# Another order of the same units in a fused attention and gated-MLP kernel

## The chip, the cores and the metric

The kernel runs on one core of a Trainium2 chip. The metric is the device time of one execution in microseconds, as the median of three executions: 165.45 us before the change (165.12 to 165.77). A profile of one execution is read beside it; its span is 164.6 us.

Five engines of the core run side by side, each with its own list of instructions that it takes in order: TensorE (PE in the profile, with its weight loads as PEld), VectorE (DVE), ScalarE (ACT), GpSimd (POOL) and SyncE (SP). GpSimd and SyncE also issue the DMA transfers.

## The reference, cut to what matters

Four batches, eight heads, a sequence of 768 and a head dimension of 64. Keys and values are mixed between eight blocks of 96 rows by a small matrix P that five rounds of normalization make nearly doubly stochastic; then comes attention inside each block, and then a gated MLP whose gate mixes the whole sequence.

```python
P = sort_net                                   # (4, 8, 8, 8)
for _ in range(5):
    P = np.exp(P - P.max(-1, keepdims=True))
    P = P / (P.sum(-1, keepdims=True) + 1e-9)
    P = P / (P.sum(-2, keepdims=True) + 1e-9)
k_sb = einsum("bhij,bhjcd->bhicd", P, k_b)     # blocks of k and of v, mixed
v_sb = einsum("bhij,bhjcd->bhicd", P, v_b)
attn = softmax(q_b @ k_sb.T / 8)               # inside each block of 96
x = attn @ v_sb                                # heads side by side: (4, 768, 512)
h = relu(x @ w_in)                             # w_in: 512 x 1024
u, v = h[..., :512], h[..., 512:]
v_n = (v - mean(v)) / sqrt(var(v) + 1e-6)
v_s = einsum("ts,bsd->btd", w_spatial, v_n) + b_spatial[None, :, None]
out = (u * v_s) @ w_out
```

## The kernel before

The kernel is a list of units, the string ORDER. Each unit is a small function that emits the instructions of one piece of work on the engines concerned, and the string is walked from left to right. So the order in the string is the order of the instructions on each engine; between engines only data and buffers tie them together. The arguments after a unit's name are mostly the PSUM bank, the engine that copies the result (A ScalarE, D VectorE, P GpSimd), the batch and the piece.

The units, in the words that this document uses:

- `L`, `LH`: a load of q, k or v of a batch (`LH` of half the heads), or of a weight (`wv` and `wu` the two halves of w_in, `ws` w_spatial, `wo` w_out). GpSimd issues all of them. q, k and v have two buffers each, so batch 2 reuses the buffers of batch 0.
- `SK`: a round of the normalization of P (exponential on ScalarE, the rest on VectorE); the last one also gives its transpose p_t. `PR`: the products that spread P over the partitions. `P0`: the masked mixing weights of batch 0, on VectorE. `PD`: those of the other batches, on GpSimd.
- `DM`: dummy matmuls on a tile of zeros whose result nobody reads.
- `QT`: transposes of q. `KT`, `VT`: mixing and transposing k, and v of batch 0. `VX`, `VM`, `VC`: the way of v into the layout that attention wants, `VC` being copies from SBUF to SBUF that SyncE issues. `QX`: transposing q of batches 2 and 3 by DMA.
- `SC`: scores and their exponential. `AT`: attention times v and its division (with P, ScalarE copies first and GpSimd multiplies). `XT`, `XX`: transposing x on TensorE, or by DMA.
- `VP`, `LN`, `LA`: the v half of h and its normalization. `UP`: the u half. `WS`: transposes of w_spatial. `SP`, `SH`: the product with w_spatial, the bias and the gate. `OP`, `OH`: the product with w_out, and the store.
- `WT`: a copy of one element on GpSimd, which makes GpSimd wait for a transposed tensor before it issues what stands behind.

The parts that the change and the prediction touch, with the order's first lines (cuts are marked):

```python
ORDER = """
IN LH:q:0:0:4 L:k:0:0:128 ID SK:0 MK SK:0 SK:0 QT:0:D:0:0:2 IV:1 QT:2:A:0:1:2 SK:0 DM:2:12:192
DM:0:12:192 SK:1 DM:2:12:192 SX DM:0:12:192 IV:0 PR:2 P0:1:0:4 L:v:0:0:128 P0:0:0:4 P0:1:4:8 P0:0:4:8
PC:A DM:7:5:384 KT:0:A:0:1:2 KT:3:D:0:0:2 ...
"""                                            # cut: 29 more lines

def load(x, b, lo, hi):
    src = {"q": q, "k": k, "v": v}[x]
    if (x, b) not in st:
        alloc(b, x)
    nc.gpsimd.dma_start(
        out=st[x, b][lo:hi],
        in_=_raw_ap(src, b * H * S * D + lo * G * D, [[G * D, hi - lo], [S * D, H], [1, G * D]]),
    )

def u_DM(ps, n, w):
    t = ps_tile(ps)
    for _ in range(int(n)):
        nc.tensor.matmul(t[:, 0, 0:int(w)], lhsT=warm[:, 0:128], rhs=warm[:, 0:int(w)], start=True, stop=True)

def u_PR(ps):
    st["pr"] = ps_tile(ps)[:, 0, 0:NB * BH].rearrange("p (x i y) -> p x i y", x=2, i=NI)
    for ih in range(2):
        for ii in range(NI):
            nc.tensor.matmul(
                st["pr"][:, ih, ii, :], lhsT=sel[:, ii, :], rhs=p_t[:, ih, :], start=True, stop=True)

def u_P0(ih, lo, hi):
    ih, lo, hi = int(ih), int(lo), int(hi)
    n = hi - lo
    pr = st["pr"][:, ih]
    nc.vector.tensor_mul(
        out=pd[0][:, lo:hi, ih * 64:ih * 64 + 64].rearrange("p h (i t) -> p h i t", t=TB),
        in0=_raw_ap(mask16, 0, [mask16.ap[0], [0, n], [0, NI], [1, TB]]),
        in1=_raw_ap(pr, lo, [pr.ap[0], [1, n], [BH, NI], [0, TB]]),
    )

def u_PD(b, lo, hi):
    b, lo, hi = int(b), int(lo), int(hi)
    n = hi - lo
    nc.gpsimd.tensor_mul(
        out=pd[b][:, lo:hi].rearrange("p h (i t) -> p h i t", t=TB),
        in0=_raw_ap(mask16, 0, [mask16.ap[0], [0, n], [0, NB], [1, TB]]),
        in1=_raw_ap(prep_sb, b * H + lo, [prep_sb.ap[0], [1, n], [BH, NB], [0, TB]]),
    )

def u_QT(ps, eng, b, hp, ih):
    b, hp, ih = int(b), int(hp), int(ih)
    lo, n = (0, 128) if ih == 2 else (ih * 64, 64)
    t = ps_tile(ps).rearrange("p x c -> p (x c)")
    for g in range(G):
        for hh in range(2):
            nc.tensor.matmul(
                t[hh * 64:hh * 64 + 64, g * n:(g + 1) * n],
                lhsT=st["q", b][lo:lo + n, 2 * hp + hh, g * D:(g + 1) * D],
                rhs=ident[lo:lo + n, lo:lo + n],
                start=True, stop=True,
            )
    copy(
        eng,
        q_tile(b, hp)[:, lo * G:(lo + n) * G].rearrange("p (x g) -> p x g", g=G),
        t[:, 0:n * G].rearrange("p (g x) -> p x g", g=G),
    )

# ... cut: KT, VT, VX

def u_VM(ps, eng, b, hp):
    b, hp = int(b), int(hp)
    t = ps_tile(ps)
    for hh in range(2):
        nc.tensor.matmul(
            t[:, hh, 0:G * D], lhsT=pd[b][:, 2 * hp + hh, :], rhs=st["v", b][:, 2 * hp + hh, :],
            start=True, stop=True,
        )
    copy(
        eng,
        vm[b % 2][:, :, 2 * hp:2 * hp + 2, 0:D].rearrange("p g h d -> p h g d"),
        t[:, :, 0:G * D].rearrange("p h (g d) -> p h g d", g=G),
    )

def u_VC(b, ih):
    b, ih = int(b), int(ih)
    for i in range(ih * NI, ih * NI + NI):
        src = vm[b % 2][i * TB:(i + 1) * TB]
        dst = vb[b % 2][:, i]
        nc.sync.dma_start(
            out=dst.rearrange("c h d -> c (h d)"),
            in_=src.rearrange("t g h d -> t g (h d)"),
        )

def u_WT(x, b, ih):
    b, ih = int(b), int(ih)
    src = st["qX", b][0:1, 0, 0:1] if x == "q" else x_tile(b, ih)[0:1, 0, 0:1]
    nc.gpsimd.tensor_copy(out=gate[0:1, 0:1], in_=src)

def u_OH(ps, eng, b, c):
    b, c = int(b), int(c)
    t = ps_tile(ps)
    for mc in range(FC):
        nc.tensor.matmul(
            t[:, 0, :], lhsT=st["gt", b, mc][:, c * 128:(c + 1) * 128], rhs=w_out_sb[:, mc, :],
            start=(mc == 0), stop=(mc == FC - 1),
        )
    o_sb = moe.tile([128, DM], FP32, name="oh_sb", tag="oh", bufs=3)
    copy(eng, o_sb, t[:, 0, :])
    nc.sync.dma_start(out=out[b, c * 128:(c + 1) * 128, :], in_=o_sb)
```

Of the kernel before, what the change touches and what calls it, by code (L numbers as in the profile page):

```python
# [13 lines left out]


ORDER = """
IN LH:q:0:0:4 L:k:0:0:128 ID SK:0 MK SK:0 SK:0 QT:0:D:0:0:2 IV:1 QT:2:A:0:1:2 SK:0 DM:2:12:192
DM:0:12:192 SK:1 DM:2:12:192 SX DM:0:12:192 IV:0 PR:2 P0:1:0:4 L:v:0:0:128 P0:0:0:4 P0:1:4:8 P0:0:4:8
PC:A DM:7:5:384 KT:0:A:0:1:2 KT:3:D:0:0:2 KT:5:A:0:3:2 VT:2:A:0:1 LH:q:0:4:8 VT:7:D:1:1 L:wv
VT:0:D:2:1 SC:3:0:1:1 KT:5:D:0:2:2 VX:7:A:0:1 VX:0:D:1:1 SC:1:0:0:1 QT:3:A:0:2:2 VT:7:D:2:0 PD:3:0:4  # L20
AT:5:D:0:1:1 VT:0:A:3:1 QT:1:A:0:3:2 PD:1:4:8 L:wu VX:7:D:2:1 AT:3:D:0:0:1 L:ws PD:3:4:8 SC:5:0:2:1
VX:0:A:3:1 VX:7:D:2:0 VT:1:D:0:0 SC:3:0:3:1 AT:5:D:0:2:1 VT:7:D:1:0 L:v:1:0:128 VT:0:A:3:0 SC:1:0:1:0
AT:3:D:0:3:1 XT:5:D:0:1:0 PD:2:0:4 SC:6:0:0:0 VX:0:A:0:0 L:k:1:0:128 VX:1:D:3:0 PD:1:0:4 PD:2:4:8
VX:2:A:1:0 XT:3:D:0:1:1 SC:6:0:2:0 AT:4:D:0:0:0 SC:0:0:3:0 L:q:1:0:128 VP:3:A:0:5 AT:6:P:0:2:0
VP:4:D:0:3:4 L:wo AT:6:P:0:3:0 WS:0:A:2 UP:2:A:0:1:1 AT:4:D:0:1:0 WS:0:A:1 UP:6:A:0:0:1 L:v:2:0:128
VM:2:D:1:0 VM:0:A:1:3 XT:4:D:0:0:0 WS:5:A:5 L:k:2:0:128 XT:7:D:0:0:1 VM:2:A:1:1 LN:0:3:6 VM:0:D:1:2
L:q:2:0:128 WS:4:D:3 L:v:3:0:128 VP:7:A:0:2 KT:0:A:1:0:2 KT:2:A:1:2:2 KT:4:A:1:3:2 LA:P:0:5
VP:6:A:0:0:1 WS:0:A:0 UP:4:A:0:1:0 QT:6:D:1:3:2 LN:0:0:3 QT:2:A:1:1:2 LA:P:0:4 VC:1:1 QT:0:D:1:2:2
UP:4:A:0:0:0 KT:6:D:1:1:2 SC:2:1:3:1 QT:0:D:1:0:2 LA:P:0:3 SC:4:1:2:1 LA:P:0:0 SC:6:1:1:1 WS:2:D:4
VC:1:0 AT:0:D:1:3:1 LA:P:0:1 SC:4:1:0:1 AT:2:D:1:2:1 BB SC:6:1:1:0 VM:0:A:2:0 AT:4:D:1:1:1 SC:6:1:0:0  # L30
AT:2:D:1:0:1 LA:P:0:2 AT:0:P:1:1:0 SC:4:1:3:0 AT:6:D:1:0:0 SP:2:D:0:1 SC:6:1:2:0 XX:1:1 AT:4:P:1:3:0
SP:0:P:0:0 AT:4:P:1:2:0 VM:6:A:2:2 QX:D:2 SP:2:D:0:3 VM:4:A:2:1 XX:1:0 VM:6:A:2:3 VC:2:1 VC:2:0
SP:0:D:0:2 WT:x:1:0 L:k:3:0:128 VM:6:A:3:0 VM:2:A:3:1 VM:4:D:3:2 UP:0:A:1:0:1 UP:2:A:1:1:1
KT:0:D:2:2:2 KT:4:A:2:3:2 KT:6:A:2:1:2 KT:2:D:2:0:2 VM:0:A:3:3 OP:4:D:0:2 SC:0:2:0:1 SC:2:2:3:1
VP:6:A:1:4:5 AT:2:P:2:3:1 AT:0:P:2:0:1 L:q:3:0:128 VP:4:D:1:0:1 SC:2:2:3:0 SC:6:2:2:0 LN:1:4:6
VP:0:A:1:2:3 SC:6:2:1:1 SC:4:2:1:0 LA:P:1:5 OP:2:A:0:1 LA:P:1:4 AT:6:D:2:3:0 OP:0:A:0:0 AT:2:D:2:2:0
AT:4:P:2:1:0 UP:6:D:1:0:0 LN:1:0:4 VC:3:0 SC:2:2:0:0 SC:4:2:2:1 UP:0:A:1:1:0 LA:D:1:1 LA:D:1:2
AT:2:D:2:0:0 KT:6:A:3:3:2 LA:D:1:0 LA:P:1:3 KT:4:A:3:2:2 XX:2:0 KT:0:D:3:1:2 KT:2:A:3:0:2 QX:D:3
SP:6:D:1:2 AT:2:P:2:1:1 AT:0:D:2:2:1 SP:4:D:1:0 SP:6:P:1:1 VP:0:D:2:0:1 UP:4:A:2:1:0 SP:6:D:1:3
SC:4:3:0:0 SC:0:3:2:0 XX:2:1 VP:2:D:2:2:3 SC:0:3:1:0 SC:4:3:2:1 UP:6:A:2:0:0 AT:0:D:3:0:0 LN:2:0:4  # L40
VP:2:A:2:4:5 UP:6:A:2:1:1 LA:P:2:2 AT:0:P:3:2:0 AT:2:P:3:1:0 LA:D:2:1 LA:D:2:3 UP:4:A:2:0:1 LN:2:4:6
LA:D:2:0 SC:0:3:3:0 LA:D:2:5 VC:3:1 SC:6:3:0:1 LA:P:2:4 OP:2:D:1:2 OP:4:A:1:1 AT:2:D:3:3:0 XX:3:0
AT:6:D:3:2:1 SP:0:P:2:1 SC:6:3:1:1 SC:2:3:3:1 OP:4:A:1:0 AT:2:D:3:1:1 AT:6:D:3:0:1 SP:0:P:2:3
AT:2:D:3:3:1 XX:3:1 UP:6:D:3:0:0 SP:0:D:2:2 UP:6:A:3:1:0 SP:0:D:2:0 VP:6:A:3:0:1 VP:0:A:3:2:3
OP:6:A:2:1 LN:3:0:4 LA:D:3:1 VP:0:A:3:4:5 LA:D:3:2 UP:6:A:3:1:1 LN:3:4:6 LA:P:3:5 UP:2:A:3:0:1
LA:P:3:3 LA:D:3:4 LA:D:3:0 OP:6:A:2:2 OP:0:D:2:0 SP:6:D:3:1 SP:0:D:3:2 SP:6:P:3:0 SH:0:D:3:3:0
SH:1:D:3:3:1 OH:0:A:3:0 OH:7:A:3:2 OH:1:A:3:1 OH:0:A:3:3 OH:7:A:3:4 OH:1:A:3:5
"""


# [593 lines left out]
```

## Time and profile before

| what | value |
|---|---|
| time, median of 3 | 165.45 us |
| span of the profiled execution | 164.6 us |
| TensorE busy | 145.4 us (88%), 1593 matmuls |
| VectorE busy | 112.4 us (68%) |
| ScalarE busy | 87.3 us (53%) |
| GpSimd busy | 56.0 us (34%) |
| DMA packets | 36690, 25.50 MB |

How to read it: [...] The chain of waits is followed back from the last instruction, at each step to what released it. A line such as L289 is a line of the kernel: L261 `PR`, L268 `P0`, L280 `PD`, L289 `DM`, L296 `WS`, L323 `QT`, L338 `KT` and `VT`, L389 `VM`, L422 `SC`, L447 `AT`, L535 `UP`, L547 `SP`, L582 `OH`; L107 and L109 are the helper that copies on ScalarE and on VectorE, and L155 the helper of the loads.

### The profile page before, as it was taken

What the parts mean: (1) busy time and instruction counts of PE and PEld (TensorE: products, weight loads), DVE (VectorE), ACT (ScalarE), POOL (GpSimd) and SP (SyncE); (2) the same over time, 40 slices, a digit from 0 to 9 for tenths busy, and PEclk for the clock granted to TensorE, in tenths of its full rate; (3) what the DMA queues carried; (4) which work ended last, traced back from release to release, by engine and by line L of the source; (5) the groups of instructions that cost most, each with busy time, mean ns of one, the idle gap of its engine ahead of it and who ended that gap; (6) DMA issues with size and microseconds to landing.
All of it is one profiled execution on the core that took longest, in us unless ns stands there. A gap on an engine that the chain in (4) does not pass through costs nothing.

```text
span 164.6 us, 3884 instructions
## 1 busy us (share of the span) xinstructions
PE 145.4 (88%) x1593; PEld 91.5 (56%) x1593; DVE 112.4 (68%) x225; ACT 87.3 (53%) x135; POOL 56.0 (34%) x77
## 2 busy tenths in 40 slices
...
GB/s 16 202 203 204 81 137 208 205 203 205 209 250 255 203 201 191 130 192 95 203 239 204 312 189 199 105 4 0 0 295 187 96 0 0 131 127 127 0 208 178
DMA packets 36690, 25.50 MB, mean 155 GB/s; under 512 B 16576, under 2 KB 33472, under 8 KB 36672
## 3 DMA queue, kind: packets, MB, share of 16 engines
...
q8 instruction: 12, 0.20, 0.5%
q14 instruction: 6, 0.05, 0.1%
...
## 4 chain that ended last, share of the span: by engine, by line
PE 62%; DMA 21%; DVE 7%; ACT 3%; issue 2%; SPq 1%; POOLq 1%; POOL 1%; ACTq 0%; DVEq 0%
PE ps L547 14%; DMA v_in<-in_v_dram 10%; PE ps L490 10%; PE ps L535 10%; PE ps L596 7%; PE ps L289 4%; PE ps L447 4%; PE ps L422 4%; DMA xT<-x_sb 4%; DMA q_in<-in_q_dram 3%; DMA vb<-vm 3%; DVE z L553 2%; PE ps L338 2%; PE ps L582 2%; PE ps L389 2%
## 5 line engine op out<-in xcount | busy, mean ns | idle before, releaser
L547 PE MATMUL ps<-wspT,v_sb 128*128 128x384 bf16 x180 | 32.0, 332 | 0.0
L435 ACT ACTIVATE ex<-ps 96x768 bf16<-96x768 f32 x32 | 24.6, 806 | 10.7 <-PE ps L422 10.6
L535 PE MATMUL ps<-xT,w_in_sb 128*128 128x384 bf16 x128 | 23.1, 326 | 1.2 <-DVE z L553 1.1
L547 PEld LDWEIGHTS <-v_sb 128*128 128x128 bf16 x180 | 17.5, 100 | 11.6 <-issue 0.8
L459 POOL TENSOR_TENSOR x_sb<-xr,rec 96x512 bf16<-96x512 f32 x11 | 11.7, 1069 | 34.6 <-DVE rec L458 30.6
L490 PE MATMUL ps<-w_in_sb,xT 128*128 128x512 bf16 x96 | 22.7, 380 | 0.0
L504 DVE BATCH_NORM_STATS2 stats<-v_sb 128x6 f32<-128x512 bf16 x24 | 16.3, 679 | 9.1 <-ACT v_sb L113 8.9
L113 ACT ACTIVATE u_sb<-ps 128x768 bf16<-128x768 f32 x14 | 11.3, 809 | 17.8 <-PE ps L535 10.2
L553 DVE TENSOR_TENSOR z<-ps,b_bc 128x768 f32<-128x768 f32 x15 | 14.3, 955 | 7.3 <-PE ps L547 7.3
L535 PEld LDWEIGHTS <-w_in_sb 128*128 128x128 bf16 x128 | 11.9, 98 | 9.2 <-issue 1.3
L596 PE MATMUL ps<-w_out_sb,gt 128*128 128x512 bf16 x72 | 16.7, 379 | 0.0
L459 DVE TENSOR_TENSOR x_sb<-ps,rec 96x512 bf16<-96x512 f32 x21 | 14.4, 687 | 0.7
L559 POOL TENSOR_TENSOR gt<-z,u_sb 128x768 bf16<-128x768 f32 x5 | 8.2, 1643 | 17.9 <-DVE z L553 17.9
L490 PEld LDWEIGHTS <-xT 128*128 128x128 bf16 x96 | 8.7, 98 | 9.3
L447 PE MATMUL ps<-vb,ex 96*128 96x65 bf16 x256 | 12.6, 197 | 1.2 <-DMA vb<-vm 1.2
L447 PEld LDWEIGHTS <-ex 96*128 96x128 bf16 x256 | 11.0, 100 | 4.6 <-issue 1.6
L521 POOL TENSOR_SCALAR v_sb<-v_sb,nm,rstd 128x512 bf16<-128x512 bf16 x13 | 10.5, 811 | 3.9 <-ACT rstd L512 2.5
L596 PEld LDWEIGHTS <-gt 128*128 128x128 bf16 x72 | 6.7, 98 | 7.5
L113 ACT ACTIVATE v_sb<-ps 128x1024 bf16<-128x1024 f32 (+1 forms) x9 | 8.4, 931 | 4.2 <-PE ps L490 4.0
L520 POOL TENSOR_SCALAR nm<-mv 128x1 f32<-128x1 f32 x13 | 2.7, 207 | 22.2 <-DVE mv L505 22.2
L422 PEld LDWEIGHTS <-kT 64*96 64x96 bf16 x256 | 7.8, 122 | 4.3 <-issue 3.3
L280 POOL TENSOR_TENSOR pd<-mask,prep_sb 128x512 bf16<-128x512 bf16 x6 | 6.5, 1102 | 10.6 <-ACT prep_sb L107 10.5
...
## 6 DMA issues: line engine op xcount, KB each, us to landing
...
k_in<-in_k_dram POOLq DMA_DIRECT2D x4, 768.0 KB, 12.2
...
```

The source lines that it names most:

```text
L113: nc.scalar.activation(out=out, in_=in_, func=AF.Relu)
L422: nc.tensor.matmul(t[0:BLK, hh, ii * 128:ii * 128 + BLK], lhsT=kT[rows, i * BLK:(i + 1) * BLK], rhs=rhs, start=True, stop=True,)
L435: nc.scalar.activation(out=dst, in_=src, func=AF.Exp, scale=scale)
L447: nc.tensor.matmul(t[:, hh, ii * VW:ii * VW + D + 1], lhsT=e[:, c:c + 128], rhs=vb[b % 2][:, ih * NI + ii, 2 * hp + hh, 0:D + 1], start=Tr ...
L459: (nc.gpsimd if eng == "P" else nc.vector).tensor_mul(out=x_sb[:, hp].rearrange("p i (h d) -> p h i d", h=2), in0=tv[:, :, :, 0:D], in1=_r ...
L490: nc.tensor.matmul(t[:, x, :], lhsT=x_tile(b, n // 3)[:, kc, n % 3 * 128:(n % 3 + 1) * 128], rhs=w_in_sb[:, kc, DH:DFF], start=(kc == 0), ...
L504: nc.vector.bn_stats(out=stats, in_=v_sb[:, x, :])
L521: nc.gpsimd.tensor_scalar(out=v_sb, in0=v_sb, scalar1=nm[:, 0:1], scalar2=rs[:, n:n + 1], op0=ALU.add, op1=ALU.mult)
L535: nc.tensor.matmul(t[:, x, 0:HW], lhsT=w_in_sb[:, kc, mc * 128:(mc + 1) * 128], rhs=x_tile(b, ih)[:, kc], start=(kc == 0), stop=(kc == KC ...
L547: nc.tensor.matmul(t[:, x, 0:HW], lhsT=st["v_sb", b, n][:, mc * 128:(mc + 1) * 128], rhs=wspT[:, n, x * HW:(x + 1) * HW], start=(n == 0), ...
L553: nc.vector.tensor_add(out=z.rearrange("p (x c) -> p x c", x=2), in0=t[:, :, 0:HW], in1=b_bc.rearrange("p (x c) -> p x c", x=2),)
L596: nc.tensor.matmul(t[:, x, :], lhsT=st["gt", b, mc][:, c * 128:(c + 1) * 128], rhs=w_out_sb[:, mc, :], start=(mc == 0), stop=(mc == FC - 1),)
```

## The change

Only the string ORDER changes; no function does, and the units are the same but for the dummies and for the engines that some of them name. What it does, and what for:

- the first half of q is followed at once by k (as it already was), and the load of v of batch 0 comes ahead of the memsets and the second half of q on GpSimd;
- the loads of the second half of w_in, of w_spatial and of v and k of batch 1 stand ahead of GpSimd's mask products (`PD`), which wait for a copy on ScalarE;
- the loads of a batch stand further ahead of their use; those of batch 3 wait (`WT`) for the transposed q of batch 2;
- the dummies in front of `PR` are 6 times 12 of 64 columns, where they were 4 times 12 of 192;
- both first `QT` copies are on ScalarE; some other copies change engine, `QX` of batch 3 goes from VectorE to GpSimd, and two of the last six output copies go to VectorE.

```diff
-IN LH:q:0:0:4 L:k:0:0:128 ID SK:0 MK SK:0 SK:0 QT:0:D:0:0:2 IV:1 QT:2:A:0:1:2 SK:0 DM:2:12:192
-DM:0:12:192 SK:1 DM:2:12:192 SX DM:0:12:192 IV:0 PR:2 P0:1:0:4 L:v:0:0:128 P0:0:0:4 P0:1:4:8 P0:0:4:8
-PC:A DM:7:5:384 KT:0:A:0:1:2 KT:3:D:0:0:2 KT:5:A:0:3:2 VT:2:A:0:1 LH:q:0:4:8 VT:7:D:1:1 L:wv
-VT:0:D:2:1 SC:3:0:1:1 KT:5:D:0:2:2 VX:7:A:0:1 VX:0:D:1:1 SC:1:0:0:1 QT:3:A:0:2:2 VT:7:D:2:0 PD:3:0:4
-AT:5:D:0:1:1 VT:0:A:3:1 QT:1:A:0:3:2 PD:1:4:8 L:wu VX:7:D:2:1 AT:3:D:0:0:1 L:ws PD:3:4:8 SC:5:0:2:1
-VX:0:A:3:1 VX:7:D:2:0 VT:1:D:0:0 SC:3:0:3:1 AT:5:D:0:2:1 VT:7:D:1:0 L:v:1:0:128 VT:0:A:3:0 SC:1:0:1:0
-AT:3:D:0:3:1 XT:5:D:0:1:0 PD:2:0:4 SC:6:0:0:0 VX:0:A:0:0 L:k:1:0:128 VX:1:D:3:0 PD:1:0:4 PD:2:4:8
-VX:2:A:1:0 XT:3:D:0:1:1 SC:6:0:2:0 AT:4:D:0:0:0 SC:0:0:3:0 L:q:1:0:128 VP:3:A:0:5 AT:6:P:0:2:0
-VP:4:D:0:3:4 L:wo AT:6:P:0:3:0 WS:0:A:2 UP:2:A:0:1:1 AT:4:D:0:1:0 WS:0:A:1 UP:6:A:0:0:1 L:v:2:0:128
-VM:2:D:1:0 VM:0:A:1:3 XT:4:D:0:0:0 WS:5:A:5 L:k:2:0:128 XT:7:D:0:0:1 VM:2:A:1:1 LN:0:3:6 VM:0:D:1:2
-L:q:2:0:128 WS:4:D:3 L:v:3:0:128 VP:7:A:0:2 KT:0:A:1:0:2 KT:2:A:1:2:2 KT:4:A:1:3:2 LA:P:0:5
-VP:6:A:0:0:1 WS:0:A:0 UP:4:A:0:1:0 QT:6:D:1:3:2 LN:0:0:3 QT:2:A:1:1:2 LA:P:0:4 VC:1:1 QT:0:D:1:2:2
-UP:4:A:0:0:0 KT:6:D:1:1:2 SC:2:1:3:1 QT:0:D:1:0:2 LA:P:0:3 SC:4:1:2:1 LA:P:0:0 SC:6:1:1:1 WS:2:D:4
-VC:1:0 AT:0:D:1:3:1 LA:P:0:1 SC:4:1:0:1 AT:2:D:1:2:1 BB SC:6:1:1:0 VM:0:A:2:0 AT:4:D:1:1:1 SC:6:1:0:0
-AT:2:D:1:0:1 LA:P:0:2 AT:0:P:1:1:0 SC:4:1:3:0 AT:6:D:1:0:0 SP:2:D:0:1 SC:6:1:2:0 XX:1:1 AT:4:P:1:3:0
-SP:0:P:0:0 AT:4:P:1:2:0 VM:6:A:2:2 QX:D:2 SP:2:D:0:3 VM:4:A:2:1 XX:1:0 VM:6:A:2:3 VC:2:1 VC:2:0
-SP:0:D:0:2 WT:x:1:0 L:k:3:0:128 VM:6:A:3:0 VM:2:A:3:1 VM:4:D:3:2 UP:0:A:1:0:1 UP:2:A:1:1:1
-KT:0:D:2:2:2 KT:4:A:2:3:2 KT:6:A:2:1:2 KT:2:D:2:0:2 VM:0:A:3:3 OP:4:D:0:2 SC:0:2:0:1 SC:2:2:3:1
  (lines left out)
-LA:D:2:0 SC:0:3:3:0 LA:D:2:5 VC:3:1 SC:6:3:0:1 LA:P:2:4 OP:2:D:1:2 OP:4:A:1:1 AT:2:D:3:3:0 XX:3:0
-AT:6:D:3:2:1 SP:0:P:2:1 SC:6:3:1:1 SC:2:3:3:1 OP:4:A:1:0 AT:2:D:3:1:1 AT:6:D:3:0:1 SP:0:P:2:3
-AT:2:D:3:3:1 XX:3:1 UP:6:D:3:0:0 SP:0:D:2:2 UP:6:A:3:1:0 SP:0:D:2:0 VP:6:A:3:0:1 VP:0:A:3:2:3
-OP:6:A:2:1 LN:3:0:4 LA:D:3:1 VP:0:A:3:4:5 LA:D:3:2 UP:6:A:3:1:1 LN:3:4:6 LA:P:3:5 UP:2:A:3:0:1
-LA:P:3:3 LA:D:3:4 LA:D:3:0 OP:6:A:2:2 OP:0:D:2:0 SP:6:D:3:1 SP:0:D:3:2 SP:6:P:3:0 SH:0:D:3:3:0
-SH:1:D:3:3:1 OH:0:A:3:0 OH:7:A:3:2 OH:1:A:3:1 OH:0:A:3:3 OH:7:A:3:4 OH:1:A:3:5
+IN SK:0 LH:q:0:0:4 L:k:0:0:128 ID MK SK:0 L:v:0:0:128 SK:0 QT:0:A:0:1:2 SK:0 QT:2:A:0:0:2 DM:0:12:64
+LH:q:0:4:8 DM:1:12:64 SX L:wv DM:0:12:64 DM:1:12:64 SK:1 DM:0:12:64 DM:1:12:64 PR:0 P0:1:4:8 IV:1
+P0:0:4:8 P0:1:0:4 P0:0:0:4 DM:7:5:384 KT:1:A:0:2:2 PC:A KT:3:A:0:3:2 VT:7:D:1:0 IV:0 VT:5:A:2:0
+KT:1:D:0:1:2 VT:0:A:3:1 KT:6:A:0:0:2 VX:3:D:1:0 SC:1:0:1:0 VX:0:D:3:1 VX:3:D:2:0 QT:4:D:0:2:2
+VT:7:A:0:1 VT:0:D:1:1 VT:1:A:0:0 SC:2:0:1:1 L:wu AT:6:D:0:1:0 L:ws SC:4:0:2:0 L:v:1:0:128 VX:0:D:0:1
+VX:1:D:1:1 L:k:1:0:128 PD:2:4:8 PD:2:0:4 QT:2:A:0:3:2 VT:7:D:2:1 AT:4:D:0:2:0 VX:0:A:0:0 SC:2:0:0:0
+AT:6:D:0:1:1 VT:0:A:3:0 SC:4:0:0:1 PD:1:0:4 AT:2:D:0:0:0 VX:0:D:3:0 SC:6:0:3:0 AT:4:D:0:0:1
+SC:2:0:3:1 PD:1:4:8 SC:0:0:2:1 L:q:1:0:128 L:wo AT:6:D:0:3:0 VX:4:D:2:1 XT:2:A:0:1:0 XT:3:D:0:0:0
+XT:7:D:0:0:1 AT:0:P:0:3:1 L:v:2:0:128 AT:4:D:0:2:1 WS:2:A:1 WS:3:A:3 VP:6:D:0:0:1 XT:0:A:0:1:1
+VP:3:D:0:2 VM:4:A:1:1 L:k:2:0:128 VM:6:A:1:0 VP:0:D:0:5 PD:3:0:4 VM:4:A:1:2 VM:1:A:1:3 LN:0:0:3
+VP:6:A:0:3:4 UP:1:A:0:0:0 L:q:2:0:128 KT:6:A:1:2:2 VC:1:0 VC:1:1 KT:4:D:1:3:2 WS:0:D:4 WS:1:A:2
+LN:0:3:6 LA:P:0:2 LA:P:0:1 UP:2:A:0:0:1 WS:7:D:5 QT:4:A:1:1:2 KT:0:D:1:1:2 KT:2:A:1:0:2 LA:D:0:3
+QT:6:D:1:0:2 QT:4:D:1:3:2 SC:0:1:1:0 UP:2:D:0:1:1 SC:0:1:0:0 LA:P:0:0 QT:6:A:1:2:2 AT:4:D:1:1:0
+SC:0:1:0:1 AT:2:D:1:0:0 SC:6:1:1:1 WS:4:D:0 SC:0:1:3:0 PD:3:4:8 AT:2:D:1:0:1 SC:6:1:2:1 LA:D:0:5
+SC:4:1:3:1 LA:P:0:4 BB AT:0:D:1:1:1 UP:2:A:0:1:0 AT:6:D:1:2:1 AT:4:P:1:3:1 SP:0:D:0:1 SC:4:1:2:0
+AT:6:P:1:3:0 SP:2:P:0:0 XX:1:1 AT:6:D:1:2:0 XX:1:0 QX:D:2 VM:4:A:2:0 SP:0:D:0:3 KT:6:A:2:1:2
+VM:4:A:2:3 SP:2:D:0:2 VM:4:A:2:1 VM:0:A:2:2 VP:6:A:1:4:5 UP:0:A:1:1:1 UP:4:A:1:0:0 KT:0:A:2:2:2
+LN:1:4:6 VC:2:0 KT:6:D:2:3:2 KT:2:D:2:0:2 VP:4:D:1:2:3 SC:2:2:2:0 SC:6:2:0:0 VC:2:1 VP:0:D:1:0:1
  (lines left out)
+WT:q:2:0 L:v:3:0:128 SC:6:2:3:1 SC:2:2:1:0 L:k:3:0:128 OP:4:A:0:2 AT:2:D:2:2:0 L:q:3:0:128 LN:1:0:4
+SP:4:D:1:2 AT:6:P:2:1:1 SP:0:D:1:3 XX:2:0 AT:4:P:2:2:1 AT:6:D:2:0:1 SP:2:D:1:1 VM:4:A:3:3 XX:2:1
+QX:P:3 SP:0:D:1:0 VM:4:A:3:2 VM:2:D:3:1 UP:6:A:2:1:0 VP:0:D:2:0:1 VM:6:A:3:0 KT:2:A:3:1:2
+SC:4:3:0:1 LA:P:2:1 SC:0:3:2:0 VC:3:0 LA:P:2:2 UP:6:A:2:0:1 SC:2:3:3:1 SC:4:3:0:0 OP:0:A:1:0 LN:2:4:6
  (lines left out)
+UP:6:D:2:1:1 LA:D:2:0 SC:2:3:2:1 SC:0:3:1:1 OP:4:A:1:1 AT:0:D:3:2:1 AT:2:D:3:1:1 SP:6:D:2:2
+SC:2:3:3:0 XX:3:1 SC:0:3:1:0 SP:4:D:2:3 AT:0:P:3:3:0 AT:2:D:3:1:0 SP:6:P:2:1 XX:3:0 SP:4:D:2:0
+UP:2:A:3:1:1 VP:4:D:3:4:5 OP:2:A:2:1 VP:4:D:3:2:3 LN:3:4:6 VP:2:A:3:0:1 UP:4:A:3:0:0 LA:P:3:5
+LA:D:3:4 UP:6:A:3:1:0 LN:3:0:4 LA:D:3:3 LA:P:3:1 LA:P:3:0 UP:4:D:3:0:1 LA:D:3:2 OP:6:A:2:2 OP:4:D:2:0
+SP:6:D:3:2 SP:4:D:3:0 SP:6:P:3:1 SH:4:D:3:3:1 SH:5:D:3:3:0 OH:7:A:3:3 OH:5:D:3:4 OH:4:A:3:0
+OH:7:D:3:5 OH:5:A:3:1 OH:4:A:3:2
```

More of the change, by code (lines that the diff above doesn't have):

```diff
@@ L33 @@
-SP:0:D:0:2 WT:x:1:0 L:k:3:0:128 VM:6:A:3:0 VM:2:A:3:1 VM:4:D:3:2 UP:0:A:1:0:1 UP:2:A:1:1:1
-KT:0:D:2:2:2 KT:4:A:2:3:2 KT:6:A:2:1:2 KT:2:D:2:0:2 VM:0:A:3:3 OP:4:D:0:2 SC:0:2:0:1 SC:2:2:3:1
[L35 to L38, printed above, removed]
@@ L39 @@
-SP:6:D:1:2 AT:2:P:2:1:1 AT:0:D:2:2:1 SP:4:D:1:0 SP:6:P:1:1 VP:0:D:2:0:1 UP:4:A:2:1:0 SP:6:D:1:3
-SC:4:3:0:0 SC:0:3:2:0 XX:2:1 VP:2:D:2:2:3 SC:0:3:1:0 SC:4:3:2:1 UP:6:A:2:0:0 AT:0:D:3:0:0 LN:2:0:4
-VP:2:A:2:4:5 UP:6:A:2:1:1 LA:P:2:2 AT:0:P:3:2:0 AT:2:P:3:1:0 LA:D:2:1 LA:D:2:3 UP:4:A:2:0:1 LN:2:4:6
-LA:D:2:0 SC:0:3:3:0 LA:D:2:5 VC:3:1 SC:6:3:0:1 LA:P:2:4 OP:2:D:1:2 OP:4:A:1:1 AT:2:D:3:3:0 XX:3:0
-AT:6:D:3:2:1 SP:0:P:2:1 SC:6:3:1:1 SC:2:3:3:1 OP:4:A:1:0 AT:2:D:3:1:1 AT:6:D:3:0:1 SP:0:P:2:3
-AT:2:D:3:3:1 XX:3:1 UP:6:D:3:0:0 SP:0:D:2:2 UP:6:A:3:1:0 SP:0:D:2:0 VP:6:A:3:0:1 VP:0:A:3:2:3
@@ new lines @@
+AT:6:P:1:3:0 SP:2:P:0:0 XX:1:1 AT:6:D:1:2:0 XX:1:0 QX:D:2 VM:4:A:2:0 SP:0:D:0:3 KT:6:A:2:1:2
+VM:4:A:2:3 SP:2:D:0:2 VM:4:A:2:1 VM:0:A:2:2 VP:6:A:1:4:5 UP:0:A:1:1:1 UP:4:A:1:0:0 KT:0:A:2:2:2
+LN:1:4:6 VC:2:0 KT:6:D:2:3:2 KT:2:D:2:0:2 VP:4:D:1:2:3 SC:2:2:2:0 SC:6:2:0:0 VC:2:1 VP:0:D:1:0:1
+WT:q:2:0 L:v:3:0:128 SC:6:2:3:1 SC:2:2:1:0 L:k:3:0:128 OP:4:A:0:2 AT:2:D:2:2:0 L:q:3:0:128 LN:1:0:4
+LA:P:1:1 AT:0:D:2:0:0 LA:P:1:0 LA:D:1:5 OP:6:A:0:1 LA:P:1:4 AT:4:P:2:3:1 UP:2:D:1:0:1 SC:6:2:3:0
+SC:0:2:0:1 LA:D:1:2 UP:4:A:1:1:0 AT:2:D:2:3:0 LA:P:1:3 AT:6:D:2:1:0 OP:0:D:0:0 SC:2:2:1:1 SC:6:2:2:1
```

2 lines of the change are left out of this document (added).

## The prediction

> **What bounds the kernel now.** I read the waits of TensorE first, because the page gives it 88% of the span; then the chain of waits up to 60 us; then TensorE's and GpSimd's timelines.
>
> The waits of TensorE (engine, line, releaser: total us, times, longest):
>
> ```profile
> PE ps L323 <- DMA q_in<-in_q_dram: 6.4, 1, 6.4
> PE ps L389 <- DMA v_in<-in_v_dram: 3.2, 1, 3.2
> PE ps L447 <- DMA vb<-vm: 1.2, 1, 1.2
> PE ps L535 <- DVE z L553: 1.1, 1, 1.1
> PE ps L582 <- POOL gt L559: 0.9, 1, 0.9
> ```
>
> The chain of waits, in order of time (start, duration, what):
>
> ```profile
> 7.90 0.81 ACT qT L107
> 8.71 0.04 issue
> 8.75 6.63 PE ps L289 x48
> 15.38 0.31 PE ps L261 x8
> ...
> 35.68 0.99 POOL x_sb L459
> 36.67 17.12 DMA v_in<-in_v_dram
> 53.79 0.05 issue
> ```
>
> Two losses stand out. (1) The 48 dummies (L289) end at 15.38 and only then do the products of the mixing weights (L261) run, though VectorE has their input p_t ready much earlier:
>
> ```profile
> 8.19 0.94 DVE L109 CAST qT<-ps 128x768 bf16<-128x768 f32 x1
> 9.06 0.20 DVE L244 TENSOR_REDUCE rowsum<-p_all 32x8 f32<-32x64 f32 x1
> ...
> 12.28 0.23 DVE L254 STREAM_TRANSPOSE p_t<-p_bf 32x64 bf16<-32x64 bf16 x1
> ```
>
> That is 12.51, so the dummies hold the start back by 15.32 - 12.51 = 2.8 us. (2) v of batch 2 is issued at 36.67, behind GpSimd's share of an attention result, and lands 17.12 us later. TensorE's timeline around it:
>
> ```profile
> 53.84 0.50 PE L389 MATMUL ps<-v_in,pd 128*128 128x384 bf16 x2 [3.17 <-DMA v_in<-in_v_dram]
> 54.17 0.41 PE L447 MATMUL ps<-vb,ex 96*128 96x65 bf16 x8
> 54.51 0.38 PE L422 MATMUL ps<-qT,kT 64*96 64x96 bf16 x8
> 54.82 1.01 PE L447 MATMUL ps<-vb,ex 96*128 96x65 bf16 x16
> ```
>
> After the gap of 3.17 us the array runs slow: the chain gives 0.94 us for 16 of the L447 matmuls (59 ns each) where it later gives 0.48 (30 ns). The recorded clock is half from 54.93 to 58.34. By the chain this costs 0.46 (those 16) + 0.18 and 0.32 (the next groups of L422 and L447) + 0.79 (L547, 2.74 for 1.95) = 1.75 us. So the late v costs 3.17 + 1.75 = 4.9 us. Apart from these two places and waits of about 1 us, TensorE is dense from 16.5 to 160.1.
>
> Why v is late: the packets of GpSimd's queue come in the order of issue, back to back. From the packet records the first half of w_in ends at 18.16, the next load starts at 21.30; v of batch 1 lands at 34.3, k at 38.2, q at 43.1, w_out at 46.6, v of batch 2 at 52.5. GpSimd's timeline shows the hole:
>
> ```profile
> 17.68 2.15 POOL L280 TENSOR_TENSOR pd<-mask,prep_sb 128x512 bf16<-128x512 bf16 x2 [10.54 <-ACT prep_sb L107]
> 19.77 0.81 POOL L206 DMA_DIRECT2D w_in_sb<-in_moe_w_in_dram  x1
> 20.57 0.84 POOL L209 DMA_DIRECT2D wsp_nat<-in_moe_w_spatial_dram  x1
> ```
>
> [...] dummies of 192 columns start 160 ns apart up to 13.97 and 83 ns after, and the slow stretch above is 3.41 us. [...] nothing runs in the 3.17 us although scores and attention stand behind. [...] v of batch 2 takes 44.7 to 52.5 (7.8 us) beside the vb copies of SyncE's queue, against 3.9 us for v of batch 0 alone.
>
> **The change part by part.**
>
> Start. The dummies become 72 of 64 columns. Cold I take 59 ns each (the 65-column rate above), warm 30: 72 x 59 = 4.2 us, or 2.2 if the clock rises early. They still start after ScalarE's first copy of qT; that copy now follows the first 12 transposes instead of the second 12, so about 8.0, and the dummies end between 10.2 and 12.2. VectorE no longer copies qT between two rounds of the normalization: rowsum of round four starts about 8.55 instead of 9.06, so p_t comes about 12.0. The products start at 12.0 to 12.3 instead of 15.3: 3.1 us earlier. Masking by VectorE then lets the first k transform start 1.2 us after the products (16.52 - 15.32 before): 13.3, a gain of 3.2.
>
> Loads. The second w_in half, w_spatial, v and k of batch 1 no longer wait for the mask products in GpSimd's order, so the hole of 3.14 us closes. At the 3.9 us of a 768 KB load: w_in ends 18.2 + 2.6 = 20.8, w_spatial 26.7 (5.9), v 30.6, k 34.5, q 38.4 alone or 41.4 if all six vb copies (0.6 MB, 3.0 us at the same rate) fall into it, w_out 44, v of batch 2 about 48. It is used later too: its first use moves behind two units of the spatial product and the rest of batch 1's attention.
>
> The rest of the order. Counted by kind, both orders have the same matmuls. With the durations that the timeline shows without a stall (spatial product 1.95 us x15, halves 0.98 x2; u 1.30 x16; v projection 0.865 x24 tiles; output 1.73 x9 and 0.865 x6; attention 0.29 x32, scores 0.28 x32, k 0.40 x16; v mix 0.33 x12, and 10.0 for the remaining 32 small units) the sum after the first k transform is 132.2 us. Before: 160.1 - 16.5 = 143.6, so 11.4 were lost: 4.9 to v, 1.05 + 1.16 + 0.20 + 0.89 to later waits, 0.58 at 26.3, and 2.6 in small stretches where ScalarE and VectorE (16.2 and 16.4 of 20 us busy from 16.5 to 36.5) hold it up.
>
> Walking the new order with these durations from 13.3, v of batch 2 is wanted at 51.3 with no loss at all and at 54 to 56 with losses: it has some 6 us of slack, and the 4.9 us should go. But what is now nearer to its load: the transposes of w_spatial wanted at 25.6 + 2 = 27.6 (landing 26.7), the first mix of v of batch 1 at 31.2 (30.6), the first q of batch 1 at 40.1 (38.4 to 41.4). I allow 1.5 us of new waits there. The later waits I leave at 3.3, the small stretches at 2.6 and the 0.6.
>
> Sum: 13.3 + 132.2 + 2.6 + 0.6 + 3.3 + 1.5 = 153.5 for the last matmul. The tail (last copy and store) was 164.6 - 160.1 = 4.5: the output copies now alternate between ScalarE and VectorE but still have three buffers, and the wait of the old tail was for a store to free one, so I leave it. Span 158.0; the timed figure was 0.85 above the span: 158.8 us. As differences: -3.2 - 4.9 + 1.5 = -6.6.
>
> **The rivals.** (a) Loads become the bound earlier: starting 3.2 us sooner with loads 3.1 to 3.7 us sooner leaves the same margin at best, and w_spatial, v and q of batch 1 could each cost 1 to 2 us. For it: the queue is full from 21.3 to 66.8 in the packet records. It would make 161 to 163. (b) The short dummies fail to raise the clock before the k transforms. [...] Cost: up to 1.7 us, 160.5. (c) The new wait is later: q of batch 3 is rearranged on GpSimd (two instructions; from 0.77 us for 512 elements about 2.3 each for 1536) where VectorE took 0.5 each undisturbed; loads of batch 3 now wait for the transposed q of batch 2. By my walk the scores that need it come about 13 us after, and 4.6 + 6.0 for its transposing DMA fits with 2 us to spare. If not, 160 to 161. (d) The stalls fall away as a more balanced order intends: later waits halve and no new ones come: 155.5 to 156.5.
>
> **Range and chances.** Only (a) with (b) or (c) brings it near 162. I predict 158.8, 156.0 to 162.2 with 8 in 10. Faster by over 2% means under 162.1: 0.89. Within 2%: 0.09. Slower: 0.02, since no work is added and both gains are plain waits.
>
> **What would show it.** Right: L261 starts at 12.0 to 12.4; no hole in GpSimd's queue near 18 to 21; no wait of L389 for v and no half clock near 55; last matmul about 153.5. Wrong: waits of L296, L389 or L323 for a DMA between 26 and 42 of more than 1.5 us together (a), k transforms at twice 0.4 us (b), L422 waiting for qX of batch 3 (c), or TensorE's waits after 60 us over 5 us.

## The result, and the profile after

The changed kernel takes 159.68 us as the median of four executions (159.00 to 159.92). Beside the kernel before the ratio is 0.963 (95% interval 0.959 to 0.968); in a later series of executions it was 0.953 (0.947 to 0.958). All ratios here are of executions within 1.5% of the fastest of their kernel, each beside the kernel before on the same chip; the kernel before spreads most (6 of 31 executions of one series lie that close), so there it is its best ones. The span of the profiled execution fell from 164.6 to 157.9 us, the last matmul from 160.1 to 153.2. In the changed kernel and in the experiments the line numbers differ by up to three from those of before, because the string has other line breaks.

The waits of TensorE after the change (the two of 0.2 us are left out):

```profile
PE ps L324 <- DMA q_in<-in_q_dram: 6.3, 1, 6.3
PE ps L448 <- DMA vb<-vm: 1.4, 3, 0.6
PE ps L491 <- DVE z L554: 1.2, 1, 1.2
PE ps L583 <- POOL gt L560: 0.6, 1, 0.6
PE ps L339 <- issue: 0.5, 1, 0.5
PE ps L290 <- ACT qT L108: 0.3, 1, 0.3
PE ps L536 <- DVE x_sb L460: 0.3, 1, 0.3
```

The wait of 3.2 us for v is gone, and no other long wait has come in its place. The granted clock is full from 12.73 us until after the last matmul. The chain of waits shows the start:

```profile
8.09 4.00 PE ps L290 x72
12.09 0.32 PE ps L262 x8
12.41 1.09 PE ps L290 x5
13.50 0.47 PE ps L339 x12
```

72 dummies of 64 columns take 4.00 us, 55.6 ns each, the pace of half clock (65 columns took 59 ns there before the change and 30 at full clock). The products (L262) start 3.3 us earlier than before, and the first k transform (L339) starts at 13.43 in TensorE's timeline, 3.1 us earlier. VectorE's timeline has the input of the products, p_t, at 11.69:

```profile
3.82 0.21 DVE L250 TENSOR_TENSOR p_all<-p_all,colsum 32x64 f32<-32x64 f32 x1
...
11.46 0.23 DVE L255 STREAM_TRANSPOSE p_t<-p_bf 32x64 bf16<-32x64 bf16 x1
```

So the dummies still hold the start back, but by 0.3 us instead of 2.8. The first line is a small extra: the same product took 0.63 us before, beside a copy of 0.60 us on GpSimd (from 3.90) that has now moved.

GpSimd's timeline shows the loads in front of the mask products (L281):

```profile
7.11 0.75 POOL L207 DMA_DIRECT2D w_in_sb<-in_moe_w_in_dram  x1
7.85 0.84 POOL L210 DMA_DIRECT2D wsp_nat<-in_moe_w_spatial_dram  x1
8.66 0.91 POOL L156 DMA_DIRECT2D v_in<-in_v_dram  x1
9.53 0.91 POOL L156 DMA_DIRECT2D k_in<-in_k_dram  x1
15.15 4.25 POOL L281 TENSOR_TENSOR pd<-mask,prep_sb 128x512 bf16<-128x512 bf16 x4 [4.71 <-ACT prep_sb L108]
```

By the packet records the queue has no hole. The last packets come at 21.6 (w_in), 27.3 (w_spatial), 31.2 (v of batch 1), 35.0 (k), 38.9 (q), 42.8 (w_out) and 49.1 (v of batch 2), each about 4 us earlier than before. That v is first used at 55.39, so there are some 6 us to spare. (For v and k the prediction gave the time by which as many bytes had moved, 34.3, 38.2 and 52.5; their last packets before the change come about 1 us later, at 35.2, 39.1 and 53.5. From here on a load lands with its last packet.)

### The profile page after: what moved, and what is told of

The parts are those of the page before. It is cut to its first block, busy times and chain, and to the rows that moved or that the text cites. A ratio compares the mean times of both kernels' runs of the same rounds, so it can differ in the third digit from the quotient of the medians.

```text
span 157.9 us, 3919 instructions
## 1 busy us (share of the span) xinstructions
PE 141.8 (90%) x1617; PEld 88.4 (56%) x1617; DVE 117.4 (74%) x231; ACT 83.5 (53%) x127; POOL 53.8 (34%) x78
## 4 chain that ended last, share of the span: by engine, by line
PE 61%; DMA 14%; DVE 12%; issue 4%; SPq 3%; ACT 2%; POOL 0%; DVEq 0%; ACTq 0%; POOLq 0%
PE ps L548 14%; PE ps L536 10%; PE ps L491 10%; DMA vb<-vm 10%; PE ps L597 8%; PE ps L448 4%; DVE z L554 4%; PE ps L339 3%; PE ps L290 3%; DMA q_in<-in_q_dram 3%; PE ps L423 3%; SPq L405 3%; DVE gt L560 2%; DVE x_sb L460 1%; DMA out_dram<-oh_sb 1%
## 5 line engine op out<-in xcount | busy, mean ns | idle before, releaser
L548 PE MATMUL ps<-wspT,v_sb 128*128 128x384 bf16 x180 | 31.2, 326 | 0.0
L460 POOL TENSOR_TENSOR x_sb<-xr,rec 96x512 bf16<-96x512 f32 x8 | 8.3, 1039 | 38.9 <-DVE rec L459 38.9
L460 DVE TENSOR_TENSOR x_sb<-ps,rec 96x512 bf16<-96x512 f32 x24 | 16.5, 687 | 0.8
L522 POOL TENSOR_SCALAR v_sb<-v_sb,nm,rstd 128x512 bf16<-128x512 bf16 x15 | 12.1, 808 | 8.5 <-issue 5.4
L114 ACT ACTIVATE u_sb<-ps 128x768 bf16<-128x768 f32 x12 | 9.7, 810 | 8.6 <-PE ps L536 8.4
L560 DVE TENSOR_TENSOR gt<-z,u_sb 128x768 bf16<-128x768 f32 x12 | 13.6, 1137 | 0.4
L108 ACT CAST vm<-ps 128x768 bf16<-128x768 f32 x11 | 8.5, 803 | 8.3 <-PE ps L390 8.3
L116 DVE TENSOR_SCALAR v_sb<-ps 128x1024 bf16<-128x1024 f32 (+1 forms) x9 | 9.9, 1101 | 3.8 <-PE ps L491 3.7
L448 PEld LDWEIGHTS <-ex 96*128 96x128 bf16 x256 | 10.1, 97 | 4.3 <-issue 1.6
L108 ACT CAST kT<-ps 128x768 bf16<-128x768 f32 x10 | 8.0, 804 | 5.7 <-PE ps L339 5.7
L108 ACT COPY o_sb<-ps 128x1024 f32<-128x1024 f32 x7 | 7.1, 1012 | 6.8 <-PE ps L597 6.6
## 6 DMA issues: line engine op xcount, KB each, us to landing
q_in<-in_q_dram POOLq DMA_DIRECT2D x3, 768.0 KB, 20.1
```

The costliest lines, as they stand in the source:

```text
L108: nc.scalar.copy(out=out, in_=in_)
L448: nc.tensor.matmul(t[:, hh, ii * VW:ii * VW + D + 1], lhsT=e[:, c:c + 128], rhs=vb[b % 2][:, ih * NI + ii, 2 * hp + hh, 0:D + 1], start=Tr ...
L460: (nc.gpsimd if eng == "P" else nc.vector).tensor_mul(out=x_sb[:, hp].rearrange("p i (h d) -> p h i d", h=2), in0=tv[:, :, :, 0:D], in1=_r ...
L522: nc.gpsimd.tensor_scalar(out=v_sb, in0=v_sb, scalar1=nm[:, 0:1], scalar2=rs[:, n:n + 1], op0=ALU.add, op1=ALU.mult)
L548: nc.tensor.matmul(t[:, x, 0:HW], lhsT=st["v_sb", b, n][:, mc * 128:(mc + 1) * 128], rhs=wspT[:, n, x * HW:(x + 1) * HW], start=(n == 0), ...
L560: eng.tensor_mul(out=gt, in0=z, in1=st["u", b, mc // 2][:, mc % 2])
```

## The experiments

The theory: the gain is the earlier start (dummies) plus the wait for v of batch 2 with the slow clock behind it, both removed by two parts of the new order (short dummies, early loads), and the rest of the order is worth nothing net. The rivals: the load stream sets the pace, so that one part alone is given back at the next load; or v was late for the place of its issue on GpSimd, as the chain of waits reads; or it is the later use of v that matters. The diffs name units moved in ORDER.

### One part at a time, in the kernel before

**Short dummies alone.**

```diff
-DM:2:12:192 DM:0:12:192 ... DM:2:12:192 ... DM:0:12:192
+DM:2:12:64 DM:0:12:64 DM:0:12:64 ... DM:2:12:64 DM:2:12:64 ... DM:0:12:64
```

> The kernel before with only the dummies replaced, 72 of 64 columns for 48 of 192. Theory (the dummies hold the start back, and the loads follow the start because GpSimd's mask products wait for it): the dummies end near 12.75, the products L261 start there instead of at 15.32, the first k transform moves from 16.52 to about 14.0, and GpSimd issues the second half of w_in 2.5 us earlier so that most of the hole in its queue closes; the wait for v of batch 2 and the slow clock stay, since the landing and the need move together. Time 2.3 to 2.9 us less. Rival (the load stream sets the pace, an earlier start is given back at v): the wait for v grows from 3.2 to over 5 us and the time falls by less than 1 us.

Measured: ratio 0.990 (0.985 to 0.996). The products start at 12.70, the first k transform at 13.90, and the second half of w_in is issued at 17.15 instead of 19.77. The wait for v stays:

```profile
PE ps L388 <- DMA v_in<-in_v_dram: 3.6, 2, 3.3
```

v lands at 51.2, 2.3 us earlier, and is wanted as much earlier. What follows: the mechanism is the theory's, the size is less sure. The ratio gives 1.6 us, below the theory; but of the executions with a granted clock of 0.979, seven of each kernel in this series, the median spans are 163.0 and 165.6 us, 2.6 apart, as the theory has it. In the profiled execution the wait is followed by 6.8 us of half clock (50.2 to 57.0) where the profile of before has 3.4, and the last matmul comes 1.9 us earlier, not 2.6.

**The four loads alone.**

```diff
-L:wv ... PD:3:0:4 ... L:wu ... L:ws ... L:v:1:0:128 ... L:k:1:0:128
+L:wv L:wu L:ws L:v:1:0:128 L:k:1:0:128 ... PD:3:0:4
```

> The kernel before with only four loads moved ahead of GpSimd's first mask product (second half of w_in, w_spatial, v and k of batch 1). Theory (v of batch 2 is late because of the order in the queue): the hole of 3.14 us closes, v of batch 2 lands near 50.6 where it is first wanted at 50.5, the wait of 3.17 us falls below 0.5 and the half clock goes: 3.1 to 4.9 us less. Rival (as the chain of waits reads, v is late because GpSimd issues it at 36.67 behind its share of attention): that issue doesn't move, so the wait stays over 2.5 us and the time within 0.5.

Measured: the time is inconclusive, ratio 0.986 (0.969 to 1.004), of four executions. The wait itself is clear: v of batch 2 lands at 45.9, even earlier than expected, and TensorE doesn't wait for it. GpSimd issues it at 38.70 here, 2.0 us later than before, and it lands 7.6 us earlier; that alone rules out the rival. But in the profiled execution other waits of TensorE came, for the copies vb and some that the profile puts down to "issue", to nothing that it shows (of these more below):

```profile
PE ps L445 <- DMA vb<-vm: 2.4, 1, 2.4
PE ps L469 <- issue: 1.2, 1, 1.2
PE ps L445 <- issue: 1.1, 1, 1.1
```

It was the longest of the four, with half clock in it (span 165.5 us, granted clock 0.979); the other three kept the full clock and have spans of 161.7 to 162.5. So the queue's order decides when v comes, and this alone shortens most executions here, but not all.

**Only the issue of that load earlier.**

```diff
-L:wo AT:6:P:0:3:0 ... L:v:2:0:128
+L:wo L:v:2:0:128 AT:6:P:0:3:0
```

> The kernel before with only the load of v of batch 2 issued earlier on GpSimd, right behind w_out and ahead of the second attention product there, so at about 34.1 instead of 36.67. Its place in the queue is the same. Theory (the queue sets the landing): v still lands at 53.8, the time stays within 0.4 us. Rival (issue plus a fixed 17.1 us, as the chain of waits can be read): it lands 2.5 us earlier and the time falls by 2 to 4 us.

Measured: issued at 33.36, 3.3 us earlier; landed at 52.3, 1.2 us earlier. But here the whole stream was earlier: the second half of w_in starts at 20.1 instead of 21.3. Against the stream v has not moved (by less than 0.1 us). The wait is 2.7 us and the ratio 1.016 (0.997 to 1.034). So the 17.12 us of the chain of waits are not a latency behind that issue; they are the place in the queue.

**Only a later use.**

```diff
-SC:6:1:1:0 VM:0:A:2:0 AT:4:D:1:1:1 ... AT:4:P:1:2:0 VM:6:A:2:2
+SC:6:1:1:0 AT:4:D:1:1:1 ... AT:4:P:1:2:0 VM:0:A:2:0 VM:6:A:2:2
```

> The kernel before with one unit moved: the first mix of v of batch 2 stands five attention and two spatial units later, right before the next mix of that batch. No load moves. Theory (the wait disappears as well if only its use moves, and with it the half clock): 3.5 to 4.9 us less, with up to 1.5 us of it given back where VectorE then waits for q of batch 2, which lands at 60.3. Rival (the load stream sets the pace, the wait only moves to the next load): 0 to 1.5 us less, with a wait of over 2 us for q, k or the transposed q of batch 2.

Measured: ratio 1.007 (1.003 to 1.011), no gain over the best executions of before; the median of all twelve is 166.11 us, that of all 31 of before 167.48. TensorE's timeline shows where the wait went:

```profile
59.14 0.81 PE L387 MATMUL ps<-v_in,pd 128*128 128x384 bf16 x4 [0.81 <-DVE z L551]
...
68.07 1.72 PE L387 MATMUL ps<-v_in,pd 128*128 128x384 bf16 x6 [3.56 <-DMA v_in<-in_v_dram]
```

The mixes of batch 2 no longer wait for their load, but those of batch 3 right behind them do, for 3.56 us, and the half clock comes there (from 69.58, 16 matmuls of L533 take 3.91 us; at full clock 8 of them take 1.30). In the kernel before they came just in time, because TensorE had been held up at batch 2. So here the rival is right in that the wait only moves to the next load, though that is v of batch 3 and none of the loads that it named. A further run moved the mixes of batch 3 too.

```diff
-... VM:6:A:3:0 VM:2:A:3:1 VM:4:D:3:2 ... VM:0:A:3:3 ... UP:6:D:1:0:0
+... VM:6:A:3:0 VM:2:A:3:1 VM:4:D:3:2 VM:0:A:3:3 UP:6:D:1:0:0
```

> The kernel before with the mixes of v moved to later places, the first of batch 2 as in the run before and the four of batch 3 right before the copies that need them; no load, no dummy moves. Theory (a wait for a load can be removed at its use as well as at its issue, if the use of the next load moves too): no wait for v over 0.5 us, no half clock, 3.0 to 4.9 us less than before. Rival (the load stream sets the pace of the whole stage): the wait turns up at k, q or the copies vb, and the time falls by less than 1.5 us.

Measured: ratio 0.994 (0.991 to 0.997). There is no wait for v, but half clock from 27.5 to 30.9, behind the wait of 1.2 us put down to "issue". The longest waits of TensorE behind the start are:

```profile
PE ps L445 <- DMA vb<-vm: 2.0, 1, 2.0
PE ps L533 <- DMA xT<-x_sb: 2.0, 2, 1.8
PE ps L469 <- issue: 1.2, 1, 1.2
...
PE ps L387 <- DVE z L551: 0.8, 1, 0.8
```

The time now goes to the copies and the transposes of x, which are DMA transfers too. In these two runs a wait that is pushed away turns up at the next transfer.

**Both parts together.** Short dummies and early loads in the kernel before, nothing else.

> The kernel before with the short dummies and the four loads moved ahead of the mask products, nothing else. Theory (these two are the change; the rest of the new order is worth nothing net): no wait for v of batch 2, no half clock after it, time within 1.5 us of the changed kernel. Rival (the later use of v of batches 2 and 3 and the loads of batch 3 behind the transposed q are needed as well): waits for v, for vb or for the transposed q of over 2.5 us together after 45 us, and 2 to 5 us more than the changed kernel.

Measured: ratio 0.953 (0.947 to 0.960), beside 0.953 (0.947 to 0.958) for the changed kernel in the same series. The last matmul ends at 153.09 and the span is 157.5. Two waits for v are left where the theory had none for batch 2, one for batch 2 and one for batch 3, 2.2 us together:

```profile
PE ps L388 <- DMA v_in<-in_v_dram: 2.2, 2, 1.1
```

So these two parts give the whole gain where the executions go well. They aren't as steady: of six executions three had spans of 160.0 to 161.5 at a granted clock of 0.973 to 0.988, where the changed kernel had two of six over 158 (158.7 and 159.7).

### One part undone, in the changed kernel

**The dummies of before.**

```diff
-DM:0:12:64 ... DM:1:12:64 ... (six of them)
+DM:0:12:192 ... DM:1:12:192 ... (four of them)
```

> The changed kernel with the dummies of before, 48 of 192 columns, in the places of its own. Theory: they start at 8.1 and take 6.4 to 7.7 us, so L261 starts at 14.5 to 15.7 and everything behind moves by 2.5 to 3.6 us: the time grows by 2.4 to 3.6 us. Rival (part of an earlier start is lost again at the loads of batch 1): less than 1.5 us.

Measured: ratio 0.964 (0.956 to 0.972), median 161.66, where the changed kernel had 159.68 and 159.17. The products start at 13.64, earlier than expected, because the clock rose at 11.3 in the profiled execution, in the middle of the dummies: the 48 take 5.70 us, before the change 6.63. It is 1.6 us later than in the changed kernel, and the last matmul 3.8 later; most of the difference is in longer waits for vb (2.2 us for 1.4) and in those put down to "issue" (1.7 for 0.5). That execution is the longest of the four. By the medians the cost is 2.0 to 2.5 us, by the ratios 0 to 1.8, so neither the theory (2.4 to 3.6) nor the rival (under 1.5) is settled; the later start is shown.

**No dummies in front at all.**

```diff
-DM:0:12:64 ... DM:1:12:64 ... (six of them)
```

> The changed kernel without its 72 short dummies (the five of 384 columns stay). Theory (the short dummies are there to raise the clock; they cost only 0.3 us of start): the products L261 start at 11.75 instead of 12.02, but the array stays at half clock [...] to 16 or 17 instead of 12.73, and the k and v transforms and first scores run slow: 0.3 less and 1 to 1.7 more, net 0.7 to 1.5 us slower. Rival (in that stage the copies of ScalarE and VectorE set the pace, not the array): within 0.4 us.

Measured: ratio 0.948 (0.943 to 0.953), span 156.6, so if anything better than with them: the four spans are 156.6 to 157.0, the ten of the changed kernel 157.1 to 159.7. The clock rises only at 15.92 (the five dummies of 384 columns take 1.71 us for 1.09), and the theory holds as far as it goes: at the 400th matmul (those 72 not counted) TensorE is 1.0 us later than in the changed kernel (29.5 to 28.5). But at the 700th it is only 0.4 later, and at the 1000th 1.0 earlier (81.6 to 82.6). The waits of TensorE tell why:

```profile
PE ps L259 <- DVE p_t L252: 4.0, 1, 4.0
PE ps L488 <- DVE z L551: 1.2, 1, 1.2
PE ps L580 <- POOL gt L557: 0.6, 1, 0.6
```

The 1.4 us for the copies vb are gone: the loss at the start is taken back there. Why the copies come in time isn't settled. In SyncE's timeline their issue around 64 us takes 5.29 us instead of 7.22, and the load of v of batch 3 starts 0.8 us later (68.0); that they hinder each other less was only argued.

**The loads behind the mask products again.**

```diff
-L:wu ... L:ws ... L:v:1:0:128 ... L:k:1:0:128 PD:2:4:8 PD:2:0:4
+PD:2:4:8 PD:2:0:4 L:wu L:ws L:v:1:0:128 L:k:1:0:128
```

> The changed kernel with the four loads put back behind GpSimd's first two mask products. Theory (with the earlier start the mask products are done by about 17.3, while the queue is busy with the first half of w_in until 18.1): the queue gets no hole over 0.5 us, landings move by less than 0.5 us, and the time stays within 0.4 us; the early start and the early loads buy the same thing. Rival (the loads' place is worth its 3 us by itself): v and w_spatial land 2 to 3 us later and the time grows by 1 to 3 us.

Measured: ratio 0.973 (0.965 to 0.981), median 162.97: 2 to 4 us worse, so my expectation was wrong and the rival right. The DMA view from 16 to 32 us (40 slices of 0.4 us: share of the engines busy, GB/s) shows the hole that I had argued away:

```profile
DMA  9999932579999999999999999999999999999999
GB/s 204 206 205 205 189 64 18 41 90 184 192 187 179 195 195 211 216 209 220 201 211 228 233 192 200 215 204 211 190 207 200 202 213 200 202 211 200 204 200 202
```

The second half of w_in is issued at 17.02, before the queue is empty, but its first packet comes at 18.91 and full rate only near 20. w_spatial lands 2.4 us later (29.7), where it is wanted:

```profile
PE ps L294 <- DMA wsp_nat<-in_moe_w_spatial_dram: 2.7, 1, 2.7
```

6.8 us of half clock follow, from 29.0 to 35.8.

### The wait for z, and a better version

The 1.2 us for z in the changed kernel are new. VectorE's timeline (first fence) and GpSimd's (second) at that place:

```profile
90.02 0.94 DVE L554 TENSOR_TENSOR z<-ps,b_bc 128x768 f32<-128x768 f32 x1
91.00 3.10 DVE L560 TENSOR_TENSOR gt<-z,u_sb 128x768 bf16<-128x768 f32 x1
94.02 0.94 DVE L554 TENSOR_TENSOR z<-ps,b_bc 128x768 f32<-128x768 f32 x1
```

```profile
90.39 2.90 POOL L179 TENSOR_SCALAR qx<-q_in 128x1536 bf16<-128x1536 bf16 x2
```

The gate product at 91.00 takes 3.10 us instead of 0.96 while GpSimd rearranges q of batch 3; the sum z at 90.02 takes its usual 0.94 us, 0.6 of it beside GpSimd. That the rearranging on GpSimd slows the product was an estimate from the 3.10 and 0.96 us; the next run takes it off GpSimd.

```diff
-QX:P:3
+QX:D:3
```

> The changed kernel with the rearranging of q of batch 3 back on VectorE. In the changed kernel VectorE's gate product at 91.0 takes 3.10 us instead of 0.96 while GpSimd rearranges q (90.4 to 93.3), and TensorE then waits 1.16 us for z. Theory (the two engines hold each other up): the product takes 0.96 again, VectorE's own rearranging about 1.0, and the wait shrinks to 0.3 or less: 0.7 to 1.3 us less. Rival (VectorE is full there anyway, so its extra work takes the place of the hold-up): within 0.4 us.

Measured: ratio 0.949 (0.943 to 0.956), median 158.66. VectorE's timeline:

```profile
90.67 0.96 DVE L557 TENSOR_TENSOR gt<-z,u_sb 128x768 bf16<-128x768 f32 x1
91.54 1.02 DVE L178 COPY qx<-q_in 128x1536 bf16<-128x1536 bf16 x2
92.48 0.95 DVE L551 TENSOR_TENSOR z<-ps,b_bc 128x768 f32<-128x768 f32 x1
```

Product and rearranging together take 1.9 us on VectorE, less than the product alone had taken, and TensorE no longer waits for z. The time is 0.5 to 1.0 us below the two medians of the changed kernel, which were measured on other chips or at other times, so its size isn't settled.

Both at once, with the changed kernel beside it on the same chip:

> The changed kernel as it is, beside the next three on one chip, as their measure. Expected span 157.1 to 158.0, the products L261 at 11.7 to 12.1, no half clock between the start and the end.

> The changed kernel without its 72 short dummies and with q of batch 3 rearranged on VectorE. Theory (both savings found so far are independent: 0.9 in the start and what follows, 1.2 at the wait for z): 1.7 to 2.3 us less than the changed kernel on the same chip. Rival [...]: only the 1.2 of z, 0.8 to 1.4 us less.

Measured: the changed kernel 159.17 us (159.01 to 161.58), the version without front dummies and with q on VectorE 157.64 (157.39 to 157.76), ratios to before 0.953 and 0.942 (0.937 to 0.946). It beats both kernels, by 1.5 us against the changed one; that lies between the theory (1.7 to 2.3) and the rival (0.8 to 1.4), so how much of it the dummies are isn't settled. The version's executions are the closest together of all: spans of 155.4 to 155.8. The profiled execution of the changed kernel wasn't as expected: it had 6.8 us of half clock, from 24.0 to 30.8, and a span of 158.7. Its wait for z is 0.4 us, not 1.2, so what that wait costs varies too.

## Why the prediction was right

- **Start.** Predicted: products at 12.0 to 12.3, first k transform at 13.3. Measured: 12.02 and 13.43. The reason given, that the dummies and not their input held it, is shown by the short dummies alone in the kernel before (12.70) and by the long ones in the changed kernel (13.64). The input came at 11.69 for the 12.0 worked out; that the two were to come together doesn't matter, since the dummies still ended last (12.09).
- **Loads.** The landings came 0.5 to 0.8 us after those worked out where no copy is in the way (21.6, 27.3, 31.2, 35.0 for 20.8, 26.7, 30.6, 34.5), and v of batch 2 at 49.1 for about 48. The hole closed, the wait for v and the half clock behind it went. Both parts alone in the kernel before gave the changed kernel's time where the executions went well. What I hadn't seen is that the later use, which I counted as additional slack, is worth little without the loads: batch 3 then waits instead.
- **New waits at 26 to 42 (1.5 us allowed).** None for a load came. w_spatial landed at 27.3 and was wanted at 27.9; with the loads put back this margin was overrun, by 2.7 us. So the place was right, and the change just avoids it. (The prediction puts rival (a) alone at 161 to 163 and then says that only (a) with another rival comes near 162; these don't agree.)
- **Later waits (3.3 us).** 1.4 for vb, 1.2 for z, 0.6 at the gate and 0.3 for x are 3.5 us. The size was right by chance: the two of before (for z at 68 us, for vb at 78) went or grew, and the one at z came from GpSimd's rearranging of q. The rival (c) had named this unit, but for another reason: it took 2.90 us, not 4.6, the scores never waited for it, and it cost 1.2 us through VectorE.
- **The clock (rival b).** The short dummies were in time: the clock rose at 12.73, before the k transforms (13.43). What raises it was not shown. But that early rise isn't needed for the time: without them it comes at 15.92, and the kernel is no slower (spans of 156.6 to 157.0 us for 157.1 to 159.7).
- **Sum.** 13.43 + 132.2 + losses = 153.22 gives losses of 7.6 us for the 8.0 worked out (the terms listed for the 132.2 add to 132.1); 4.4 of them are waits that the profile lists behind 13 us, counting the small ones. The tail took 4.7 us for 4.5.
- **The term that was off** is the last: 0.85 us from the span to the timed figure. It set a median beside the span of another execution. In the executions of both kernels the time is 1.7 to 2.0 us above the span of the same execution (159.92 and 157.9); the span itself, 158.0, was right to 0.1. Hence 159.68 for 158.8.
